# An attention and feed-forward kernel whose instruction order is planned: three edits to the attention units, one to a buffer, and a table of offsets to the planner's ranks

## The chip, the cores and the metric

The kernel runs on one core of one Trainium2 chip, in one launch. The metric is the device time of that launch in microseconds (us), timed in three runs. TensorE is called PE here, VectorE DVE, ScalarE ACT, GpSimd POOL, and SyncE, which issues most DMAs, SP.

## The reference

Attention over 4 batches of 8 heads, 768 positions of width 64. A query sees the 8 first keys ("global") and the last 96 keys up to itself ("local"), with a bias that falls with distance. The heads are laid side by side to 3072 tokens of 512 values, and a feed-forward follows.

```python
scores = scale * np.matmul(q, k.transpose(0, 1, 3, 2))
scores = np.where(keep, scores + bias, -1000000000.0)
a = np.exp(scores - np.max(scores, axis=-1, keepdims=True))
a = a / (np.sum(a, axis=-1, keepdims=True) + 1e-09)
x = np.matmul(a, v)            # heads side by side: (3072, 512)
h = x @ w_in                   # (512, 2048), doubles
g = h * np.cos(h)
out = g @ w_out                # (2048, 512), doubles
```

The two weight matrices come as 64-bit floats.

## The kernel before, in words

**Tiling.** The tokens are cut into chunks: two of 384 tokens for the first batch (chunks 0 and 1, four blocks of 96 each), then for each further batch two of three blocks and one of two (chunks 2 to 10; 4, 7 and 10 have two blocks). Every chunk has four attention units, one for each pair of heads. After attention, each chunk goes through the feed-forward in steps over the 2048 hidden columns: chunks 0 and 1 in 16 steps of 128 columns each (chunk 0 does four, chunk 1 all sixteen, chunk 0 the rest), the others in eight steps of 256. The first product of a step is "M1" (line 973); it lands in one of two PSUM banks (`ph`), and ACT, DVE, ACT, DVE make h*cos(h) of it (turn 991, angle 994, cosine 997, product 1030 or 1096), then a rounded part and a rest. The second product is line 986 for chunks 0 to 2, and from chunk 3 on a form with seven block products instead of eight (line 1191), which reads sums of the output weights that are kept in DRAM and streamed back. Each matmul of a product is done as three of rounded parts and rests.

**An attention unit.** PE makes the scores (663 or 667), DVE copies the causal half over (685) and takes bias and minimum (694), ACT takes the exponential with its sum (719), DVE adds 1e-9 and takes the reciprocal (727, 730), POOL divides (743, 748), PE transposes (847, two blocks at a time), and the transposed weights go from PSUM to SBUF as two tiles: one for the product with the preceding block's keys and the global ones, one for the own block's. Then PE multiplies by the values (890): the "burst", whose matmuls use 64 of the array's columns, two side by side. ACT or DVE copies the result to `xmem` (297, 299), DVE the rest (938). In chunks named in `DIFFER` (4 to 10) the first tile is a plain copy by ACT or DVE (`every`), and the burst takes differences of neighbouring value blocks (`vd`, line 821) with the second tile; in the others DVE masks the first tile (`others`, line 858) and no differences are made. Two-block chunks put two head pairs into one burst; `MERGE` names further chunks that do so, and is empty.

**The order.** Nothing runs in source order. Every operation is put on a list with its possible engines, its estimated cost, what it waits for, which buffers it uses and, for some, a time by which it is due. The planner gives every operation a rank (`o.key`, its latest start; line 158) and then walks through time: a free engine takes the ready operation of lowest rank whose buffers are free, a choice among engines going by waiting time and cost. The program holds each engine's instructions in that order, so each engine's queue is fixed. The planner's cost of one M1 part is 348 ns, a burst's 160 ns for each pair of matmuls; a change of array form costs 170 ns. In the first 45 us of planned time PE's gaps are filled with matmuls on zeros ("idle<-zeros", line 1518), 250 ns each.

**Buffers that matter here.** From chunk 4 on, attention has two of the eight PSUM banks for scores, transposes and burst results (`att`); chunks 2 and 3 have three. A chunk's finished rows wait in an SBUF tile `oo` for the DMA to the output; before chunk 3 that tile is taken from the class `wu` (two places, shared with weight conversion and the sums), afterwards from `oo` (two places).

Of the kernel before, what the change touches and what calls it, by code (L numbers as in the profile page):

```python
# [26 lines left out]
R = 96  # L27
# [39 lines left out]
MERGE = tuple(range(11, 11))  # L67
DIFFER = tuple(range(4, 11))
# [3 lines left out]
TAIL = 0.8  # L72

# [32 lines left out]
class Plan:  # L106
# [12 lines left out]
    def __init__(self, places, free):  # L119
        self.ops = []  # L120
        self.places = {c: list(v) for c, v in places.items()}
        self.busy = {}
        self.free = dict(free)
        self.port = 0
        self.mode = None
        self.last = {}

# [5 lines left out]
    def op(self, engines, emit, after=(), uses=(), due=None, table=None, extra=0, port=False, mode=None):  # L133
        o = Op(engines, emit, after, list(uses), due, table, extra, port, mode)
        for a in o.after:
# [137 lines left out]
class Net:  # L273
# [143 lines left out]
    def plan_weight(self, src, out, at, place, n, due):  # L417

        nc, p = self.nc, self.plan
        raw = Slot(f"w {place}", lambda i: self.const.tile([P, n, 2], U32, name="raw", tag=i))  # L420
# [53 lines left out]
        o = p.op({DVE: part(600)}, wjoin, [o], [raw, wu], port=True)  # L474
        o = p.op({ACT: part(525), DVE: part(335), POOL: part(595)}, whigh, [o], [raw, wu], port=True)
        return p.op({DVE: part(600), POOL: part(1260)}, wrest, [o], [raw, wu], due=due, port=True)

    def plan_combined(self, q):
# [11 lines left out]
        done = [[x] + self.prev.get("sums", []) for x in done]  # L490
# [99 lines left out]
    def plan_unit(self, L, pr):  # L590
# [134 lines left out]
        def add(e):  # L725
            x = st.tile[:, n2 : 2 * n2]
            nc.vector.tensor_scalar(x, x, 1e-9, None, op0=ALU.add)

        def rec(e):
            nc.vector.reciprocal(st.tile[:, 2 * n2 : 3 * n2], st.tile[:, n2 : 2 * n2])  # L730
# [69 lines left out]
    def plan_values(self, u):  # L800
# [18 lines left out]
        def step(e):  # L819
            x = vs.tile[:R, :, hs]  # L820
            self.eng(e).tensor_tensor(
                vd.tile[:, pos + lead0 : pos + nb], x[:, lead0 + 1 : nb + 1], x[:, lead0:nb], op=ALU.subtract)
# [6 lines left out]
        for ts in u["groups"]:  # L829
# [37 lines left out]

            def whole(e, pt=pt, pv=pv):
# [8 lines left out]
            ready.append(p.op({DVE: 70 + w * 104 // 100}, own, [o], [pt, pv]))  # L877
# [28 lines left out]
        def burst(e):  # L906
# [4 lines left out]
            {PE: 160 * (2 * nb - u["first"]) * len(units)}, burst, [o for x in units for o in x[3]],  # L911
# [87 lines left out]
    def plan_step(self, s, m, q, a, b):  # L999
# [10 lines left out]
        for i in range(2):  # L1010
            f = 2 * q + i
            for kk in range(self.NK):

                def m1(e, kk=kk, f=f, i=i):
# [3 lines left out]
                    {PE: 348}, m1, self.xdone[m, kk] + [self.wdone[f][0]], [ph, *xs, self.weight["wi", f]],  # L1018
# [100 lines left out]
    def plan_fast(self, s, m, q, rr, gg, product, g, due):  # L1119
# [54 lines left out]
        for i, (bank, half, left, right, k) in enumerate(jobs):  # L1174
# [12 lines left out]
            def times(e, b=b, half=half, left=left, right=right, ends=half == 1 or bank == "D"):  # L1187
# [7 lines left out]
                {PE: 348}, times, after, uses + side, due=due + (i + 1) * 348,  # L1195
# [65 lines left out]
    def plan_store(self, m, t, po, o, keep, due):  # L1261
# [5 lines left out]
        else:  # L1267
            cls = "part" if keep else "wu" if m < FAST else "oo"
# [176 lines left out]
    def windows(self):  # L1445
# [17 lines left out]
        self.weight, self.saved, self.stored = {}, {}, {}  # L1463
        p = self.plan
# [13 lines left out]
        for n in self.order:  # L1478
            for b2 in range(self.NP // UB):
                L = self.plan_loads(n, b2)  # L1480
                for i in range(UB):
                    self.plan_values(self.plan_unit(L, b2 * UB + i))
        for f in range(self.NF):
            self.wdone[f] = self.plan_weights(f)
        for q in range(NQ):
            self.plan_combined(q)
        for s, (n, i, a, b) in enumerate(self.seq):
            (self.plan_opening if n < len(OPEN) else self.plan_step)(s, n, i, a, b)
        flag = self.plan_flag()
# [105 lines left out]
```

## Time and profile before

| | |
|---|---|
| timed runs | 678.24 us median of 3 (677.9 to 679.14) |
| span of the profiled execution | 676.7 us, first to last instruction |
| what lies around the span, by the median | 1.6 us |
| busy | PE 663.8, PE weight loads 626.7, DVE 554.6, ACT 508.7, POOL 391.0 us |
| granted TensorE clock | 0.998 of full speed over the span |

Busy time of an engine is what its records cover. Matmuls overlap: a matmul of 256 columns has a record of about 280 ns, but the next one starts some 117 ns after it. So PE's busy share says that something was in the array, not that matmuls started as fast as they could; for that one reads the starts in the timeline. The profile's own span and the timed median differ by 1.6 us of launch and end.

### The profile page before, as it was taken

The numbers are of one execution on the slowest core, as the hardware profiler recorded it, in microseconds if no ns is written. First come the engines' busy times: TensorE is split into PE (matmuls) and PEld (weight loads), VectorE is DVE, ScalarE is ACT, GpSimd is POOL, SyncE is SP. The second block draws the span as 40 slices with busy tenths as digits, with TensorE's granted clock in tenths as the row PEclk, the third lists the DMA queues.
The fourth block names the chain that finished last, engine by engine and source line by source line (L and its number), as shares of the span: only waits on it lengthen the run. The fifth ranks groups of instructions, "written<-read, shape, count | busy, mean of one in ns | idle before, by whom it ended". The sixth has DMA issues, their size and how long they took to land. (4 is left out here: it accounts for less than half of the span.)

```text
span 676.7 us, 17496 instructions
## 1 busy us (share of the span) xinstructions
PE 663.8 (98%) x5810; PEld 626.7 (93%) x5810; DVE 554.6 (82%) x1726; ACT 508.7 (75%) x1253; POOL 391.0 (58%) x576
## 2 busy tenths in 40 slices
PE   8999999999999999999999999999999999999995
PEld 4769999999999998999999999999999999999995
DVE  7999898978898897777778888797878898887664
ACT  7999997579776785866778878676787788684432
POOL 5896544437457553467866776736876768532201
PEclk9999999999999999999999999999999999999999
DMA  8999200044546665877887867787687777665664
GB/s 279 336 321 380 80 1 1 22 159 121 163 139 194 221 183 174 239 220 203 244 240 207 249 213 231 245 239 232 210 240 219 235 228 235 199 224 187 191 226 150
DMA packets 86291, 136.69 MB, mean 202 GB/s; under 512 B 9904, under 2 KB 33968, under 8 KB 86192
## 3 DMA queue, kind: packets, MB, share of 16 engines
q1 hardware_dynamic: 86048, 135.23, 64.7%
q8 instruction: 48, 0.79, 0.5%
q14 instruction: 51, 0.42, 0.2%
q10 hardware_dynamic: 144, 0.26, 0.1%
HBM read 118.67 MB, written 16.78 MB: 200 GB/s over the span
## 5 line engine op out<-in xcount | busy, mean ns | idle before, releaser
L973 PE MATMUL bank<-xmem,w 128*128 128x256 f32 (+1 forms) x2112 | 344.4, 295 | 0.1
L973 PEld LDWEIGHTS bank<-xmem,w 128*128 128x128 f32 x2112 | 294.1, 189 | 7.7 <-issue 0.9
L719 ACT ACTIVATE tt<-tt,st 96x104 f32<-96x104 f32 (+1 forms) x256 | 94.6, 371 | 7.2 <-DVE st L694 6.5
L997 ACT ACTIVATE rr<-rr,half_pi 128x512 f32<-128x512 f32 (+1 forms) x104 | 71.6, 691 | 23.3 <-DVE rr L994 22.1
L986 PE MATMUL bank<-w,gh 128*128 128x256 f32 (+1 forms) x384 | 88.3, 320 | 0.0
L991 ACT ACTIVATE rr<-bank 128x512 int32<-128x512 f32 (+1 forms) x104 | 57.9, 558 | 30.9 <-PE bank L973 29.1
L1191 PE MATMUL bank<-ws,sh 128*128 128x256 f32 x384 | 75.8, 284 | 1.3 <-DVE oo L299 1.3
L994 DVE SCALAR_TENSOR_TENSOR rr<-rr,bank 128x512 f32<-128x512 int32 (+1 forms) x104 | 66.5, 639 | 8.2 <-ACT rr L991 7.6
L784 POOL TENSOR_TENSOR qk<-raw,qk 64x304 fp32r<-64x304 f32 (+1 forms) x57 | 50.0, 880 | 28.4 <-ACT qk L297 6.9
L748 POOL TENSOR_TENSOR tt<-tt,st 96x416 f32<-96x416 f32 (+1 forms) x60 | 45.4, 764 | 35.3 <-DVE sf L1137 9.1
L986 PEld LDWEIGHTS bank<-w,gh 128*128 128x128 f32 x384 | 62.7, 188 | 1.1
L1030 DVE TENSOR_TENSOR rr<-bank,rr 128x512 f32<-128x512 f32 x72 | 49.3, 684 | 16.6 <-ACT rr L997 16.4
L986 PE MATMUL bank<-w,gl 128*128 128x256 f32 (+1 forms) x192 | 61.1, 318 | 0.0
L1191 PEld LDWEIGHTS bank<-ws,sh 128*128 128x128 f32 x384 | 58.6, 188 | 2.0 <-issue 1.4
L297 ACT CAST gh<-rr 128x384 fp32r<-128x384 f32 (+1 forms) x76 | 39.5, 520 | 25.8 <-DVE rr L1030 10.8
L694 DVE CUSTOM_DVE_ANT_0 tt<-bank,dd 96x104 f32<-96x104 f32 (+1 forms) x256 | 55.0, 256 | 2.2
L1191 PE MATMUL bank<-ws,sl 128*128 128x256 f32 x192 | 54.1, 282 | 0.1
L997 ACT ACT_TABLE_LOAD x40 | 51.3, 1283 | 0.7
L719 ACT ACT_TABLE_LOAD x39 | 50.0, 1283 | 0.7
L445 POOL TENSOR_SCALAR raw<-raw 128x512 bf16<-128x512 bf16 (+1 forms) x32 | 36.6, 1167 | 23.6 <-DVE w L466 13.2
L667 PE MATMUL bank<-qk 128*96 128x200 f32 (+1 forms) x384 | 49.1, 257 | 0.0
L1191 PE MATMUL bank<-w,gh 128*128 128x256 f32 x256 | 48.7, 282 | 0.0
(137 smaller groups left out, 1532.4 us busy)
## 6 DMA issues: line engine op xcount, KB each, us to landing
ws<-sum SPq DMA_DIRECT2D x256, 256.0 KB
raw<-in_qk_dram SPq DMA_DIRECT2D x48, 174.0 KB
raw<-in_w_in_dram SPq DMA_DIRECT2D x16, 512.0 KB
sum<-sw SPq DMA_DIRECT2D x64, 128.0 KB
raw<-in_qk_dram SPq DMA_DIRECT2D x48, 150.0 KB
raw<-in_qk_dram SPq DMA_DIRECT2D x48, 148.0 KB
out_dram<-oo SPq DMA_DIRECT2D x23, 256.0 KB
raw<-in_w_out_dram SPq DMA_DIRECT2D x16, 256.0 KB
```

Of the source, the lines that this page charges most:

```text
L667: nc.tensor.matmul(out, qs[:, m, q0], ks[:, k : k + w], start=m == 0, stop=m == 1)
L694: nc.vector.tensor_tensor_reduce(tt[t // 2].tile[:, t % 2, j, :w], ps.tile[:R, i * WIN : i * WIN + w], self.dd[:, v, :w], op0=ALU.add, op1 ...
L719: nc.scalar.activation(x, x, AF.Exp, bias=st.tile[:, c : c + 1], scale=-1.0, accum_out=st.tile[:, n2 + c : n2 + c + 1])
L748: self.eng(e).tensor_tensor(x, x, r.broadcast_to([R, na, SLOT]), op=ALU.mult)
L784: self.eng(e).tensor_tensor(ks[D:, k0:k1], raw.tile[D:, k0:k1], ks.bitcast(F32)[D:, k0:k1], op=ALU.subtract)
L973: self.nc.tensor.matmul(ph, self.wi[f][:, w, kk * P : (kk + 1) * P], xx[:, kk, :], start=kk == 0 and m == 0, stop=kk == self.NK - 1 and m ...
L986: self.nc.tensor.matmul(out, gg, w[:, i, :], start=start and m == 0 and h == 0, stop=stop and m == 2)
L991: self.nc.scalar.activation(r.bitcast(I32), ph, AF.Copy, scale=1.0 / TWO_PI, bias=0.25)
L994: self.nc.vector.scalar_tensor_tensor(r, r.bitcast(I32), -TWO_PI, ph, op0=ALU.mult, op1=ALU.add)
L997: self.nc.scalar.activation(r, r, AF.Sin, bias=self.half_pi)
L1030: {DVE: dve(512)}, lambda e: nc.vector.tensor_tensor(r(), h(), r(), op=ALU.mult), [o], [ph, rr],
L1191: nc.tensor.matmul(out, x, y, start=q == 0 and j == 0 and half == 0, stop=q == self.NF // 2 - 1 and j == 2 and ends)
```

## The change

It does six things. (1) `MERGE` names chunks 2 to 10, so their three-block units also go two head pairs to a burst. (2) `DIFFER` takes in chunks 0 and 1: they make value differences and copy the first tile plainly. (3) In chunks 0 and 1 (`APART`) the add and the reciprocal are done for each pair of blocks, not once a unit. (4) Chunk 2's output tile comes from `oo`, not `wu`. (5) The planner's costs: 354 for an M1 or second-product part, 168 for a pair of burst matmuls; the first weight sums wait for the 24th-last weight that was joined. (6) Each operation has a name, and a table of 615 offsets (in ns) is added to the ranks. `COPIED` is empty, so its code does nothing.

```diff
-MERGE = tuple(range(11, 11))
-DIFFER = tuple(range(4, 11))
+BEHIND = -24
+MERGE = tuple(range(2, 11))
+DIFFER = (0, 1) + tuple(range(4, 11))
+COPIED = ()
+APART = (0, 1)
+ORDER = {
+    "u0.0 high": -45860, "v0.1 glob": -1510, "u0.1 fold": -540, "u0.1 exp": -28590, "u0.1 op2": 810,
...
+}
-            o.key = (o.due - min(o.engines.values()), i)
+            o.key = (o.due - min(o.engines.values()) + ORDER.get(o.name, 0), i)
-        done = [[x] + self.prev.get("sums", []) for x in done]
+        done = [[x] + self.prev.get("sums", self.joined[BEHIND:]) for x in done]
-        o = p.op({DVE: 85}, add, exps, [st], port=True)
-        o = p.op({DVE: 120}, rec, [o], [st], port=True)
+        ends = None
         u["norm"] = []
         for ts in groups:
             h, na = ts[0], 2 * len(ts)
+            if n in APART or ends is None:
+                cs = (2 * h, 2 * h + na) if n in APART else (0, n2)
+                ends = [x for ((t, _), _), x in zip(ttr, exps) if t in ts or n not in APART]
+                o = p.op({DVE: 85}, lambda e, cs=cs: add(e, *cs), ends, [st], port=True)
+                o = p.op({DVE: 120}, lambda e, cs=cs: rec(e, *cs), [o], [st], port=True)
-            {PE: 160 * (2 * nb - u["first"]) * len(units)}, burst, [o for x in units for o in x[3]],
+            {PE: 168 * (2 * nb - u["first"]) * len(units)}, burst, [o for x in units for o in x[3]],
-            cls = "part" if keep else "wu" if m < FAST else "oo"
+            cls = "part" if keep else "wu" if m < FAST - 1 else "oo"
```

**PE, two neighbouring units of chunk 5.** Before, each head pair has its own burst (890; `vd` are the value differences), with first products (973) and second products (1191) between:

```order
L973 MATMUL bank<-xmem,w 128x256 x6
L890 MATMUL bank<-pv,v 64x96 x4
L890 MATMUL bank<-pv,vd 64x96 x2
L890 MATMUL bank<-pv,v 64x96 x2
L890 MATMUL bank<-pv,vd 64x96 x2
L973 MATMUL bank<-xmem,w 128x256 x6
L1191 MATMUL bank<-ws,gh 128x256 x2
L1191 MATMUL bank<-ws,gl 128x256
L973 MATMUL bank<-xmem,w 128x256 x12
L667 MATMUL bank<-qk 96x96 x2
```

After, the same chunk (1031 is the burst, 1332 the second product):

```order
L1332 MATMUL bank<-w,gl 128x256
L1031 MATMUL bank<-pv,v 64x96 x4
L1031 MATMUL bank<-pv,vd 64x96 x2
L1031 MATMUL bank<-pv,v 64x96 x2
L1031 MATMUL bank<-pv,vd 64x96 x2
L1031 MATMUL bank<-pv,v 64x96 x4
L1031 MATMUL bank<-pv,vd 64x96 x2
L1031 MATMUL bank<-pv,v 64x96 x2
L1031 MATMUL bank<-pv,vd 64x96 x2
L1332 MATMUL bank<-w,gh 128x256 x2
L1332 MATMUL bank<-w,gl 128x256
```

Two units' ten matmuls each stand in one run of twenty (the trace has two records for each of them). Over the whole program the runs of burst matmuls go from 38 to 26. Eighteen second-product matmuls follow this one before the next scores. Of the matmuls on zeros 48 become 34; all other counts on PE stay.

**ACT, the middle of the opening.** Before (435 is a weight conversion, 991 and 997 turn and cosine, 719 the exponentials, 297 copies: `gh` the rounded part of h*cos(h), `xmem` attention's result):

```order
L991 ACTIVATE rr<-bank 128x384 x2
L435 ACTIVATE raw<-raw 128x512
L997 ACT_TABLE_LOAD
L997 ACTIVATE rr<-rr,half_pi 128x384
L297 CAST xmem<-bank 128x384
L719 ACT_TABLE_LOAD
L719 ACTIVATE tt,st<-tt,st 96x104 x8
L297 CAST gh<-rr 128x384
L997 ACT_TABLE_LOAD
L997 ACTIVATE rr<-rr,half_pi 128x384
L719 ACT_TABLE_LOAD
L719 ACTIVATE tt,st<-tt,st 96x104 x8
```

After (1138 cosine, 848 exponentials, 424 copies, 563 a weight conversion; `pv` are the transposed weights):

```order
L848 ACTIVATE tt,st<-tt,st 96x104 x3
L1138 ACT_TABLE_LOAD
L1138 ACTIVATE rr<-rr,half_pi 128x384
L424 CAST w<-wu 128x512
L848 ACT_TABLE_LOAD
L848 ACTIVATE tt,st<-tt,st 96x104
L424 COPY pv<-bank 104x384
L848 ACTIVATE tt,st<-tt,st 96x104 x6
L424 COPY pv<-bank 104x384
L848 ACTIVATE tt,st<-tt,st 96x104
L563 ACTIVATE raw<-raw 128x512
L848 ACTIVATE tt,st<-tt,st 96x104 x3
```

One excursion to the cosine is gone and copies of `pv` stand between the exponentials. Counted up to the 64th exponential, the last of chunks 0 and 1, ACT has 14 copies of `pv` more (ten of 104x384, four of 104x192) and one of `xmem` more; it has two table loads, two scalings of the queries, one turn, one cosine and three conversions of line 435 (one of 512, two of 256 columns) fewer. Up to the same chunks' last `xmem` rest, DVE loses all 16 masked copies of line 858 (twelve 104x384, four 104x192) and gains five `vd` and eight more pairs of add and reciprocal; POOL gains three `vd`.

## Rows read from the trace of the kernel before

**Rows 1.** First part of the page: busy us (share of the span) xinstructions

```profile
PE 663.8 (98%) x5810; PEld 626.7 (93%) x5810; DVE 554.6 (82%) x1726; ACT 508.7 (75%) x1253; POOL 391.0 (58%) x576
```

**Rows 2.** Windows: stretch, its us, then each engine's busy time, clock, DMA

```profile
12.00:62.00 50.00, 48.28 (x499) 36.47 (x500) 46.48 (x205) 49.71 (x163) 41.53 (x49) 1.00 0.99 345
62.00:100.00 38.00, 38.00 (x227) 35.98 (x227) 33.74 (x59) 38.00 (x87) 19.29 (x19) 1.00 0.28 93
100.00:200.00 100.00, 99.99 (x716) 93.84 (x715) 86.36 (x247) 77.71 (x182) 49.26 (x69) 1.00 0.31 96
```

**Rows 3.** Waits of PE after 60 us: total us, times, longest

```profile
PE bank L1191 <- DVE oo L299: 1.3, 1, 1.3
PE bank L847 <- DVE pv L299: 0.7, 1, 0.7
```

**Rows 4.** Timeline of PE around one three-block burst: start, us, what

```profile
364.18 0.40 PE L1191 MATMUL bank<-ws,gh 128*128 128x256 f32 x2
364.42 0.28 PE L1191 MATMUL bank<-ws,gl 128*128 128x256 f32 x1
364.62 0.39 PE L890 MATMUL bank<-pv,v 104*64 104x96 f32 x4
364.84 0.34 PE L890 MATMUL bank<-pv,vd 96*64 96x96 f32 x4
...
365.77 0.99 PE L973 MATMUL bank<-xmem,w 128*128 128x256 f32 x6
366.60 0.54 PE L667 MATMUL bank<-qk 128*96 128x200 f32 x4
```

**Rows 5.** Timeline of PE around a burst that holds two head pairs

```profile
423.14 0.39 PE L890 MATMUL bank<-pv,v 104*64 104x96 f32 x4
...
424.62 0.63 PE L973 MATMUL bank<-xmem,w 128*128 128x256 f32 x3
```

**Rows 6.** Timeline of DVE and of SP's queue before 270 us

```profile
269.27 0.69 DVE L299 COPY oo<-bank 128x512 f32<-128x512 f32 x1 [1.92 <-DMA out_dram<-oo]
...
264.66 5.69 SPq L1283 DMA_DIRECT2D out_dram<-oo  x2
```

**Rows 7.** Timeline of PE: fillers in the opening, and what follows

```profile
8.49 3.41 PE L1518 MATMUL idle<-zeros 128*128 128x512 bf16 x15
12.05 0.51 PE L847 MATMUL bank<-ident,tt 96*96 96x96 f32 x4
```

**Rows 8.** Groups by form, first 80 us: busy us, mean ns

```profile
L858 DVE SCALAR_TENSOR_TENSOR pv<-own,bank 104x384 f32<-104x384 f32 x12 | 6.5, 545 | 0.4 <-PE bank L847 0.3
L618 ACT ACTIVATE raw<-raw,steep 128x384 f32<-128x384 f32 x7 | 4.3, 615 | 3.7 <-POOL small L357 2.8 <-DMA raw<-in_qo_dram 0.8
L435 ACT ACTIVATE raw<-raw 128x512 int32<-128x512 uint32 x18 | 11.6, 680 | 0.0
L435 ACT ACTIVATE raw<-raw 128x256 int32<-128x256 uint32 x8 | 3.3, 432 | 0.0
L997 ACT ACTIVATE rr<-rr,half_pi 128x384 f32<-128x384 f32 x8 | 4.9, 616 | 0.0
L991 ACT ACTIVATE rr<-bank 128x384 int32<-128x384 f32 x9 | 4.3, 487 | 0.0
L297 ACT CAST xmem<-bank 128x384 fp32r<-128x384 f32 x6 | 2.8, 464 | 0.0
L997 ACT ACT_TABLE_LOAD x3 | 3.8, 1283 | 0.1
```

**Rows 9.** Groups by form, whole span: ACT's copies of the transposed weights

```profile
L297 ACT COPY pv<-bank 104x384 f32<-104x384 f32 x15 | 7.1, 476 | 3.7 <-DVE pv L864 3.6
L297 ACT COPY pv<-bank 104x192 f32<-104x192 f32 x18 | 5.4, 318 | 4.7 <-PE bank L847 2.5 <-DVE pv L864 2.0
```

**Rows 10.** Instructions of the value differences on DVE

```profile
L821 DVE TENSOR_TENSOR vd<-v x1: 543/543/543, 538.8 to 538.8; 96x384 f32<-96x384 f32 x1
```

**Rows 11.** Timeline of DVE after the burst of Rows 4

```profile
366.97 0.52 DVE L938 TENSOR_TENSOR xmem<-bank,xmem 128x224 fp32r<-128x224 f32 x2
```

More of the change, by code (lines that the diff above doesn't have):

```diff
@@ L126, in __init__ @@
         self.last = {}
+        self.part, self.count = "", {}
     def drained(self, o, e):
@@ L134, in op @@
         o = Op(engines, emit, after, list(uses), due, table, extra, port, mode)
+        name = emit.__name__
+        if name == "<lambda>":
+            self.count[self.part] = self.count.get(self.part, 0) + 1
+            name = f"op{self.count[self.part]}"
+        o.name = f"{self.part} {name}"
         for a in o.after:
@@ L419, in plan_weight @@
         nc, p = self.nc, self.plan
+        p.part = place
         raw = Slot(f"w {place}", lambda i: self.const.tile([P, n, 2], U32, name="raw", tag=i))
@@ L723, in plan_unit, with add, rec @@
             exps.append(p.op({ACT: 365}, exp, [o], [tt[t // 2], st], table="exp"))
-        def add(e):
-            x = st.tile[:, n2 : 2 * n2]
+        def add(e, a, b):
+            x = st.tile[:, n2 + a : n2 + b]
             nc.vector.tensor_scalar(x, x, 1e-9, None, op0=ALU.add)
-        def rec(e):
-            nc.vector.reciprocal(st.tile[:, 2 * n2 : 3 * n2], st.tile[:, n2 : 2 * n2])
-        o = p.op({DVE: 85}, add, exps, [st], port=True)
-        o = p.op({DVE: 120}, rec, [o], [st], port=True)
+        def rec(e, a, b):
+            nc.vector.reciprocal(st.tile[:, 2 * n2 + a : 2 * n2 + b], st.tile[:, n2 + a : n2 + b])
+        ends = None
         u["norm"] = []
@@ L821, in step @@
             self.eng(e).tensor_tensor(
-                vd.tile[:, pos + lead0 : pos + nb], x[:, lead0 + 1 : nb + 1], x[:, lead0:nb], op=ALU.subtract)
+                vd.tile[:, pos + lead0 : pos + nb], x[:, lead0 + 1 - low : nb + 1 - low], x[:, lead0 - low : nb - low], op=ALU.subtract)
         w = (nb - lead0) * P
@@ L866, in own, with mine @@
                 )
+            def mine(e, pv=pv, a=a, na=na, z0=z0):
+                self.eng(e).tensor_tensor(
+                    wide(pv.tile[:R, 1, z0:], a, na), wide(pv.tile[:R, 0, z0:], a, na), mask(self.own[:R], a, na), op=ALU.mult
+                )
             def whole(e, pt=pt, pv=pv):
@@ L876, in plan_values @@
                 ready.append(p.op({DVE: 70 + w * 104 // 100}, others, [o], [pt, pv]))
-            ready.append(p.op({DVE: 70 + w * 104 // 100}, own, [o], [pt, pv]))
+            if n in COPIED:
+                ready.append(p.op({DVE: 70 + w * 104 // 100, POOL: 100 + w * 1125 // 512}, mine, ready[-1:], [pv], port=True))
+            else:
+                ready.append(p.op({DVE: 70 + w * 104 // 100}, own, [o], [pt, pv]))
             if lead:
@@ L1017, in plan_step @@
                 done = self.chain(f"m1 {s}", p.op(
-                    {PE: 348}, m1, self.xdone[m, kk] + [self.wdone[f][0]], [ph, *xs, self.weight["wi", f]],
+                    {PE: 354}, m1, self.xdone[m, kk] + [self.wdone[f][0]], [ph, *xs, self.weight["wi", f]],
                     due=due + (4 * i + kk + 1) * 348,
@@ L1194, in plan_fast @@
             last[bank, half] = self.chain("m2", p.op(
-                {PE: 348}, times, after, uses + side, due=due + (i + 1) * 348,
+                {PE: 354}, times, after, uses + side, due=due + (i + 1) * 348,
             ))
```

8 lines of the change are left out of this document (added), and 114 rows, old and new, of the table ORDER.

## The prediction

> **What bounds the kernel now.** I read the first part of the page first: PE is busy for 663.8 of 676.7 us [rows 1], so only what PE itself does, or the few microseconds in which it does nothing useful, can move the time. The windows then say where the others matter [rows 2]. From 12 to 62 us ACT is busy for 49.71 of 50 us and DVE for 46.48, while PE has time for fillers: this is the opening, in which attention for the first batch and the conversion of the weights both press on ACT. From 62 to 100 us PE and ACT are both full; from 100 us PE alone (99.99 of 100, ACT 77.71). The table of waits, restricted to the time after 60 us, has little: one wait of 1.3 us and one of 0.7 us that count [rows 3]. A busy PE can still be slow, so I read starts in its timeline last, around a change of array form: that is where a cost hides inside "busy" [rows 4, 5].
>
> **Bursts (a gain of 4.2 us).** Take the burst of one head pair in a three-block chunk [rows 4]. From its first start at 364.62 to the next full-width matmul at 365.77 are 1.15 us for 24 records. A burst of two head pairs with two blocks each has 32 records and takes 424.62 - 423.14 = 1.48 us [rows 5]. The eight records between them cost 0.33 us, 0.041 each, so 24 of them are 0.99 us and 0.16 us is a fixed part; the longer burst has the same (1.48 - 32 x 0.041 = 0.16): a second pair in the burst pays nothing. Around it, two plain matmuls take 364.42 - 364.18 = 0.24, 0.12 each, but the last before the burst takes 0.20, which is 0.08 too much, and the six after it take 366.60 - 365.77 = 0.83 instead of 0.72, 0.11 too much. One run of burst matmuls thus costs 0.16 + 0.08 + 0.11 = 0.35 us beyond its matmuls. Runs go from 38 to 26. Twelve times 0.35 is 4.2 us, all of it on PE after 100 us, where PE is full, so nothing hides it. Bounds: if only the fixed part inside goes, 12 x 0.16 = 1.9; at most 4.2 plus what the runs' neighbours cost, which I leave at 4.6.
>
> **Chunk 2's output tile (1.3 us).** The longest wait of PE after 60 us is that on the copy `oo` by DVE [rows 3]. DVE's own timeline shows why it is late: the copy at 269.27 waited 1.92 us for a DMA from `oo` to the output, one of the pair that SP's queue starts at 264.66 [rows 6]. Its place was still being sent. With `oo` this chunk has two places of its own class that no sum or weight uses, so the second copy needs not wait for the first one's DMA. I take all 1.3 us; the lower bound is 0, if another operation of `oo` comes as late.
>
> **The opening (0.5 us).** Here the edits add and remove much, so I count each queue up to the last opening exponential or rest, from the counts in the order. ACT gains ten `pv` copies of 384 columns at 0.476 and four of 192 at 0.318 [rows 9], 6.0 us, and one `xmem` copy, 0.46. It loses two table loads, 2 x 1.283 = 2.57, two query scalings, 1.23, a turn and a cosine, 0.49 + 0.62, and three conversions, 0.68 + 2 x 0.43 = 1.54 [rows 8]; together 6.45. The queue that is never idle is as long as before, so the last opening exponential comes when it came, and what follows on ACT with it. DVE loses 12 x 0.545 = 6.5 us of masked copies alone [rows 8] and gains five `vd`, one at 0.543 [rows 10] and four that are a third wider, about 0.7 each by estimate from it, 3.3 in all; eight more pairs of tiny add and reciprocal take most of the rest. The transposes need each half's reciprocal only, so the first half of a unit reaches PE earlier, and fewer gaps open: the planner puts 14 fewer fillers. In the trace 15 fillers and the way to the next transpose take 12.05 - 8.49 = 3.56 us, 0.237 each [rows 7], so 14 are 3.3 us. That is the upper bound of the gain. It can't all stay, because PE's first products hand over to ACT through two banks, and ACT's queue has not become shorter: what PE gains at 50 us it waits for ACT by 75 us. The other bound is a loss: a `pv` copy on ACT can stand at the head of the queue and wait. Over the span 33 such copies of these two shapes sat idle for 3.7 + 4.7 us [rows 9], 0.25 each; fourteen of them would cost 3.6 us. Between a gain of 3.3 and a loss of 3.6 I take a gain of 0.5, since DVE's shorter queue brings the copies' partners earlier.
>
> One rule speaks against moving `vd` to DVE. The Trainium skill, page "SBUF — State Buffer", section "SBUF: two separate sides", says that VectorE and GpSimd share one port pair as an exclusive lock, taken for a whole instruction by a VectorE operation with two inputs in SBUF, and `vd` is one. By it five `vd` would hold POOL for about 3.3 us while POOL divides. The rows show POOL with 8.5 us of 50 idle there [rows 2], and no `vd` on DVE in the opening; no run here shows the lock by itself. By the rule the opening's gain would be gone, and the sum 0.5 smaller.
>
> **Ranks (0.5 us).** The offsets reorder PE after 100 us: first products run further ahead of their second products, so angle, cosine and sums have more time. What is left there to gain by the waits is 0.7 us [rows 3], plus small ones that no row of that view holds. I take 0.5; bounds are a gain of 2.5 us and a loss of 2.5, since a new order can put an operation before its input. The costs 354 and 168 only shape the plan. The copies of `xmem` that a merged burst brings all come at once, on ACT and DVE that have 22 and 14 us of 100 idle [rows 2].
>
> **The sum.** 4.2 + 1.3 + 0.5 + 0.5 = 6.5 us off a span of 676.7 is 670.2. The median of the timed runs is 1.6 us above the span, 678.24. With the same 1.6 us, the prediction is 671.7.
>
> **Rivals.** *The opening's gain stays.* If ACT's copies find their transposes ready and PE keeps its 3.3 us, and the 0.7 us of [rows 3] goes too, the time is 678.24 - 4.2 - 1.3 - 3.3 - 0.9 = 668.5. For it: 14 fillers fewer; against it: ACT's 49.71 of 50 [rows 2]. Chance 0.18.
>
> *The merged bursts give it back.* From chunk 4 on a merged burst takes both attention banks, and no scores or transposes can start until the copies are out. In the trace a bank is free at 366.97 + 0.52 = 367.49, 1.7 us after PE went on at 365.77 [rows 4, 11]; two pairs need two more copies, another 0.5 us. In the order 18 second-product matmuls at 0.12 stand behind the burst shown, 2.1 us, and at some bursts fewer. If PE waited 0.5 us after each of 12, 6.0 us would come back and with the rest of the sum unchanged it would be 677.7: no change. Against it: PE has enough other work in between at most places. Chance 0.09.
>
> *Slower: ACT's copies block the opening.* A `pv` copy and DVE's masked copy read the same bank, and the copy waits for the other: 3.6 us before the 15 wide ones [rows 9]. If each of the 14 new ones waits for a transpose and for DVE, with its own length, 0.476 + 0.25 = 0.73 us, and the two table loads and the rest that pay for them in my count were waited for anyway, ACT is 14 x 0.73 = 10.2 us late at 62 us, and PE, fed by ACT's turns through two banks, is too. 678.24 - 4.2 - 1.3 + 10.2 = 682.9. It decides the sign from a net delay of about 7 us on. For it: ACT is full to 100 us. Against: the same copies as a mask stood on DVE, itself nearly full, and the table loads do go. Chance 0.07.
>
> *The lock* of the paragraph above, as a mechanism: POOL's divisions wait for DVE's `vd`, five times about 0.66 us, and the gain of the opening turns into a loss of 0.5: 672.7. Chance 0.06.
>
> **How the numbers follow.** The forecast has 0.60, with its own range 668.9 to 674.5. A change of 0.2%, 1.36 us, is about what can be told from none. Faster than 676.9: the forecast, the first rival and the lock, 0.84, and a part of the second, 0.02, so 0.86. Within 0.2%: the rest of the second rival, 0.07. Slower: 0.07. The range for 8 in 10 goes from 667.0, a bit below the first rival by the upper bounds of ranks and bursts, to 676.8, where the bounds of opening and ranks, 3.6 and 2.5 lost, would leave 678.24 - 4.2 - 1.3 + 3.6 = 676.3 with ranks at 0.
>
> **What would show it.** Bursts: 26 runs of burst matmuls, a run of 40 records taking about 40 x 0.041 + 0.16 = 1.8 us, and the matmul after it starting as before. Output tile: no wait of PE on `oo` near 270 us, and no wait of DVE on a DMA there. Opening: the 64th exponential within 1.5 us of where it was, 34 fillers, ACT still full from 12 to 62 us, and PE's saturation not earlier by more than 2 us. Ranks: waits of PE after 60 us below 1.5 us in all. I am wrong if scores or transposes wait for a bank after merged bursts, if ACT has idle time before `pv` in the opening, or if PE is seen waiting between 62 and 100 us for ACT.

## The result and the profile after

The changed kernel takes 686.19 us (median; 685.21 to 686.93) against 678.31 us of the kernel before in the same session: a ratio of 1.0113, 95% interval 1.0098 to 1.0127. It is slower by 7.9 us where 6.5 us less were forecast. The profiled execution has a span of 684.6 us against 676.7.

The first part of the page of the changed kernel answers [rows 1]:

```profile
PE 664.1 (97%) x5796; PEld 629.8 (92%) x5796; DVE 554.4 (81%) x1737; ACT 505.8 (74%) x1263; POOL 396.1 (58%) x579
```

Every engine's work is what it was, within some 5 us (PE 663.8 to 664.1, ACT 508.7 to 505.8, POOL 391.0 to 396.1). What grew is PE's idle time, span less busy: from 12.9 to 20.5 us, nearly all of the loss. That PE's busy time did not fall, with 14 fillers fewer and twelve bursts joined, is in part the halved clock described below, under which its matmuls take longer. The windows say where. They answer [rows 2]; the columns are the stretch and its us, busy us of PE, PEld, DVE, ACT and POOL with instructions, PE's granted clock, the DMA share, GB/s.

```profile
12.00:62.00 50.00, 45.91 (x467) 35.41 (x464) 42.84 (x202) 47.31 (x165) 33.20 (x42) 0.93 0.97 319
62.00:100.00 38.00, 37.50 (x222) 35.01 (x222) 34.79 (x63) 37.66 (x84) 15.38 (x16) 1.00 0.38 127
100.00:200.00 100.00, 99.48 (x697) 93.29 (x697) 87.28 (x239) 77.74 (x197) 60.95 (x77) 1.00 0.31 96
...
300.00:400.00 100.00, 97.42 (x914) 95.55 (x913) 83.23 (x274) 77.91 (x197) 63.52 (x96) 1.00 0.78 226
...
500.00:600.00 100.00, 97.43 (x930) 94.99 (x929) 83.07 (x257) 74.93 (x173) 58.49 (x83) 1.00 0.77 223
```

The two last stretches in the kernel before, same columns:

```profile
300.00:400.00 100.00, 99.10 (x935) 96.41 (x935) 78.55 (x263) 77.16 (x201) 72.11 (x117) 1.00 0.75 222
...
500.00:600.00 100.00, 100.00 (x950) 98.22 (x949) 84.97 (x267) 78.52 (x196) 69.88 (x104) 1.00 0.78 232
```

Two losses are to be seen. In the opening ACT, which had 0.3 us of 50 idle, has 2.7, and PE's clock is 0.93 instead of 1.00. And late in the program, in the two stretches shown, PE stands idle 2.6 us of 100, where it had been idle for 0.9 and not at all. From 200 to 300 us it is the other way round (1.5 us idle before, none now); over 100 to 600 us PE's idle time goes from 2.4 to 6.4 us.

**How much of it is the opening.** A count of what PE has done by 100 us tells: the windows from 0 to 100 us for one line alone (columns: busy PE, busy PEld, clock, DMA share, GB/s; the weight loads lose no record, so I count these). First products in the kernel before and in the changed one:

```profile
0.00:100.00 100.00, 35.10 (x167) 28.96 (x168) 1.00 0.70 236
```

```profile
0.00:100.00 100.00, 29.28 (x147) 25.14 (x147) 0.97 0.73 237
```

Second products stand at 135 in both. So 21 first products are missing at 100 us. One starts 0.177 us after another: in the timeline of PE before, six take 83.39 - 82.33 = 1.06 us.

```profile
82.33 1.22 PE L973 MATMUL bank<-xmem,w 128*128 128x384 f32 x6
83.39 0.40 PE L986 MATMUL bank<-w,gh 128*128 128x256 f32 x2
```

That is 21 x 0.177 = 3.7 us lost by 100 us. The other 7.9 - 3.7 = 4.2 us are lost later, in the part where bursts and the output tile should have given 4.2 + 1.3 = 5.5 us back. If they did, about 9.7 us of new waiting stands against them. The table of waits that follows holds 5.9 of these (6.8 us after 100 us, less the 0.9 that stood beside the `oo` wait before), so this sum does not show that the whole 5.5 us came.

**Which waits.** PE's waits after 60 us in the changed kernel, answering [rows 3] (total us, times, longest):

```profile
PE bank L1114 <- DVE rr L1171: 1.5, 3, 0.7
PE bank L1031 <- ACT pv L424: 1.2, 2, 0.8
PE bank L796 <- ACT pv L424: 1.2, 1, 1.2
PE bank L796 <- DVE pv L426: 0.7, 1, 0.7
PE bank L980 <- POOL tt L881: 0.6, 1, 0.6
PE bank L1127 <- ACT oo L424: 0.5, 1, 0.5
PE bank L796 <- POOL qk L917: 0.5, 2, 0.3
```

Before there were two waits that counted, 2.0 us together; the seven rows here sum to 6.2 us, all rows of that view to 7.3, and name scores (L796), bursts (L1031), transposes (L980) and first products (L1114), behind ACT, DVE and POOL. There is no single culprit. The wait on `oo` in chunk 2 is gone, as forecast.

One of these waits, followed back, shows how the new order makes them. PE, ACT and SP's queue before 398 us in the changed kernel:

```profile
393.21 0.49 PE L980 MATMUL bank<-ident,tt 96*104 96x96 f32 x4
...
397.59 0.58 PE L796 MATMUL bank<-qk 128*96 128x200 f32 x4 [1.16 <-ACT pv L424]
```

```profile
395.30 0.45 ACT L424 CAST qk<-raw 128x304 fp32r<-128x304 f32 x1 [2.86 <-DMA raw<-in_qk_dram]
...
396.97 0.47 ACT L424 COPY pv<-bank 104x384 f32<-104x384 f32 x1
```

```profile
384.45 2.81 SPq L1298 DMA_DIRECT2D ws<-sum  x5
387.48 2.39 SPq L900 DMA_DIRECT2D raw<-in_qk_dram  x4
```

Scores need a bank that holds transposed weights until ACT has copied them. The transposes ran at 393.21, but the copy only at 396.97: it stood in ACT's queue behind a conversion of `qk`, which waited 2.86 us for its load; and that load was issued behind transfers of `ws` (five in the window shown). PE waits for ACT, ACT for a DMA that has nothing to do with the copy. By the Trainium skill, page "TensorE: Matmul & The Clock Gate", section "Architectural detail: the array is 16× 32×32, not 1× 128×128", the queues of ACT and DVE are strictly first in, first out; the copy that could run and did not agrees.

**The clock.** PE's timeline at 51 us shows the burst of 32 records that should take 1.48 us:

```profile
50.55 0.51 PE L980 MATMUL bank<-ident,tt 96*104 96x96 f32 x4 [0.38 <-DVE st L823]
51.44 0.39 PE L1031 MATMUL bank<-pv,v 104*64 104x96 f32 x4 [0.38 <-ACT pv L424]
...
53.46 0.54 PE L1031 MATMUL bank<-pv,vd 96*64 96x96 f32 x4
54.16 1.04 PE L1127 MATMUL bank<-w,gh 128*128 128x256 f32 x2 [0.16 <-ACT w L424]
```

Here it takes 54.16 - 0.16 - 51.44 = 2.56 us up to the end of its last record (1.56 by that count at 423 us in the kernel before). The granted clock of 52 to 58 us is 0.50, the lower of the two levels (1.2 GHz). Ahead of it PE had stood before bank after bank from 46 us on, and of the fillers 34 are left of 48, the last at 41.9 us instead of 44.3.

**The bursts themselves** did what was forecast. A joined one of 48 records in the changed kernel, answering [rows 4, 5]:

```profile
374.13 0.39 PE L1031 MATMUL bank<-pv,v 104*64 104x96 f32 x4
374.34 0.34 PE L1031 MATMUL bank<-pv,vd 96*64 96x96 f32 x4
...
376.28 1.56 PE L1114 MATMUL bank<-xmem,w 128*128 128x256 f32 x11
```

It takes 376.28 - 374.13 = 2.15 us; 48 x 0.041 + 0.16 is 2.13. The fixed part is paid once for two pairs. Its neighbours cost what they did: in the four bursts of 48 records that have full-width matmuls on both sides and no wait, the matmul ahead takes 0.21 us and the six behind 0.81, by their starts. The timeline has 26 runs of burst matmuls.

### The profile page after: what moved, and what is told of

It is laid out like the page before. It is cut to its first block, busy times and chain, and to the rows that moved or that the text cites. A ratio compares the mean times of both kernels' runs of the same rounds, so it can differ in the third digit from the quotient of the medians.

```text
span 684.6 us, 17411 instructions
## 1 busy us (share of the span) xinstructions
PE 664.1 (97%) x5796; PEld 629.8 (92%) x5796; DVE 554.4 (81%) x1737; ACT 505.8 (74%) x1263; POOL 396.1 (58%) x579
## 4 chain that ended last, share of the span: by engine, by line
PE 72%; DVE 8%; ACT 8%; DMA 6%; POOL 3%; issue 2%; SPq 0%; POOLq 0%; ACTq 0%; DVEq 0%
PE bank L1114 32%; PE bank L1332 17%; PE bank L1127 13%; DMA raw<-in_qk_dram 4%; PE bank L796 4%; PE bank L1031 3%; ACT tt L848 2%; PE bank L980 2%; DMA v<-in_v_dram 1%; ACT pv L424 1%; DVE tt L823 1%; DVE bank L814 1%; DVE qk L907 1%; POOL qk L917 1%; DVE pv L997 1%
## 5 line engine op out<-in xcount | busy, mean ns | idle before, releaser
L1114 PE MATMUL bank<-xmem,w 128*128 128x256 f32 (+1 forms) x2112 | 309.0, 295 | 1.5 <-DVE rr L1171 1.5
L1114 PEld LDWEIGHTS bank<-xmem,w 128*128 128x128 f32 x2112 | 281.7, 189 | 5.7 <-PE bank L796 0.8
L1332 PE MATMUL bank<-ws,sh 128*128 128x256 f32 x384 | 73.7, 284 | 0.0
L917 POOL TENSOR_TENSOR qk<-raw,qk 64x304 fp32r<-64x304 f32 (+1 forms) x60 | 54.1, 907 | 28.5 <-DVE qk L907 3.4
L1127 PEld LDWEIGHTS bank<-w,gh 128*128 128x128 f32 x384 | 64.4, 192 | 5.6 <-ACT oo L424 0.9
L1171 DVE TENSOR_TENSOR rr<-bank,rr 128x512 f32<-128x512 f32 x72 | 49.0, 684 | 14.2 <-ACT rr L1138 13.8
L428 POOL TENSOR_SCALAR sh<-sf 128x512 fp32r<-128x512 f32 x43 | 27.4, 637 | 47.3 <-PE bank L1332 19.6
L814 DVE COPY_PREDICATED bank<-mine,bank 96x192 f32<-96x192 uint32 (+1 forms) x128 | 40.2, 327 | 15.0 <-PE bank L796 14.2
L796 PE MATMUL bank<-qk 128*96 128x200 f32 (+1 forms) x384 | 47.7, 257 | 3.2 <-ACT pv L424 1.2
```

Source lines behind the costliest of these rows:

```text
L796: nc.tensor.matmul(out, qs[:, m, q0], ks[:, k : k + w], start=m == 0, stop=m == 1)
L814: nc.vector.copy_predicated(w[:, :, :R], self.mine.bitcast(U32).broadcast_to([R, ni - i0, R]), w[:, :, SLOT:])
L917: self.eng(e).tensor_tensor(ks[D:, k0:k1], raw.tile[D:, k0:k1], ks.bitcast(F32)[D:, k0:k1], op=ALU.subtract)
L1114: self.nc.tensor.matmul(ph, self.wi[f][:, w, kk * P : (kk + 1) * P], xx[:, kk, :], start=kk == 0 and m == 0, stop=kk == self.NK - 1 and m ...
L1127: self.nc.tensor.matmul(out, gg, w[:, i, :], start=start and m == 0 and h == 0, stop=stop and m == 2)
L1171: {DVE: dve(512)}, lambda e: nc.vector.tensor_tensor(r(), h(), r(), op=ALU.mult), [o], [ph, rr],
```

## The experiments

The theories: **A**, the table of offsets puts operations ahead of their inputs. **B**, the joined bursts cost by what they hold (two banks, copies of two pairs at once). **C**, the opening's edits cost. **D** came after the first four runs: the plan of before is a rarely good one, and any new order, with or without a reason, opens waits that the old one had not. All times are medians of device us; ratios are to the kernel before, run beside it, with 95% intervals.

### Parts of the change alone

`no_table`: the changed kernel with an empty table.

```
-    "u0.0 high": -45860, "v0.1 glob": -1510, "u0.1 fold": -540, "u0.1 exp": -28590, "u0.1 op2": 810,
...
+ORDER = {}
```

> The changed kernel with an empty table of offsets; every other edit is in it. Theory A (the offsets cost the time: they put scores, first products and bursts ahead of their inputs, so that PE waits): the bursts' 4.2 us and the output tile's 1.3 us show, and the time is 671 to 674 us. Theory B (the merged bursts cost it, because scores and transposes wait for the banks that two head pairs hold): 682 to 686, as in the changed kernel. Theory C (the opening costs it, by value differences and sums per half unit): 681 to 685, with the granted clock of 12 to 62 us again below 1.00.

684.01 us, ratio 1.0078 (1.0064 to 1.0092). Most of the loss is there without the table. A is refuted as the main cause; the offsets account for some 2 us. The time fits both B and C, but C's clock does not: it is 1.00 from 12 to 62 us.

`merge_oo`: the kernel before with two lines of the diff.

```
-MERGE = tuple(range(11, 11))
+MERGE = tuple(range(2, 11))
-            cls = "part" if keep else "wu" if m < FAST else "oo"
+            cls = "part" if keep else "wu" if m < FAST - 1 else "oo"
```

> The kernel before with two of the edits alone: two head pairs share a burst from batch two, and chunk 2's output tile has a place of its class. No table, no new costs, the opening as before. Theory A and theory C: 12 x 0.35 + 1.3 = 5.5 us less than before, 672.8, and no wait of PE on an output copy near 270 us. Theory B: no gain, 677 to 682, with PE's scores and transposes waiting for a bank after bursts of 40 or 48 records.

682.74 us, 1.0066 (1.0052 to 1.008): 3.8 us slower, where the parts promise 5.5 less, and just above B's range. The opening is as before (168 first products by 100 us), so what is lost, 9.3 us if both terms came in full, is lost later, by joining and planning anew. PE's waits after 60 us sum to 6.6 us, against 2.2 before; they name POOL's `tt`, DVE's `rr` and `qk`, again many small ones.

`open_only`: the opening's edits alone.

```
-DIFFER = tuple(range(4, 11))
+DIFFER = (0, 1) + tuple(range(4, 11))
+APART = (0, 1)
```

> The kernel before with the opening's edits alone: value differences for the first two blocks, and sums per half unit there. Theory C: 680 to 684, with fewer fillers, PE idle from 45 to 60 us and a granted clock under 1.00 there. Theories A and B: 677 to 679, the clock 1.00 from 12 to 62 us; by the prediction's term 677.7.

682.52 us, 1.0056 (1.004 to 1.0071). The time is C's, the clock (1.00) is not: PE is idle more, without a fall. By 100 us PE had done 159 first products instead of 168, and 130 second ones instead of 135.

`table_late`: the changed kernel, the offsets of the opening left out: the names that begin with `u0`, `u1`, `v0`, `v1`, `w`, `c0` and `s0` to `s19`.

```
-    "u0.0 high": -45860, "v0.1 glob": -1510, "u0.1 fold": -540, "u0.1 exp": -28590, "u0.1 op2": 810,
...
     "v2.0 glob": -12810, "u2.0 op1": -76810, "u2.0 op2": -70080, "u2.0 khigh": -18650, "u2.0 op3": -31250,
```

> The changed kernel with the offsets of the opening left out (units and values of the first two blocks, weights, the first sum, steps 0 to 19); all later ones stay. Theory A, if the loss comes from the later offsets: 681 to 686, with PE's waits after 130 us as in the changed kernel (scores and bursts behind ACT's and DVE's copies). If it comes from the opening's offsets: 673 to 677. Theory B gives 682 to 686 in either case, theory C 681 to 685 with the clock below 1.00 in the opening.

693.95 us, 1.0219 (1.0204 to 1.0233), outside every range. Part of the table is worse than none and worse than all of it, which suggests that the offsets fit each other and the order that they make together. This, and that both parts alone (`merge_oo`, `open_only`) lose some 3.7 us, pointed to D. The delay of the first weight sums (edit 5; the code makes them wait for all of the last 24 joined weights, not for the 24th-last) was not run alone.

### The order held

To part an edit from the plan that comes with it, I wrote the plan of the kernel before down (each operation's engine and rank) and let the kernel follow that list instead of the planner. An operation whose shared bank or buffer is still taken goes next after that is free. That the order is held can be read from `held_oo` below: in its trace PE, DVE, ACT and POOL run every instruction in the order of the kernel before.

```
-        self.emit(p.run(), banks)
+        self.emit(p.replay(), banks)
```

`held_merge` has the held order and `MERGE` of the change.

> The kernel before with its whole order held by a written list (each operation with the engine and the rank that it has in the kernel before) and one edit: two head pairs share a burst from batch two, the first pair's burst records moved down to the second pair's. Nothing else moves but what the joined burst pushes back. Theory D (the edits do what they say; it is the new plan, in any version, that opens waits which the old one had not): 12 x 0.35 = 4.2 us less than before, 673 to 676. Theory B (the merged burst itself costs, by banks and copies that it holds): 677 to 682, with waits of transposes or scores right behind bursts of 40 and 48 records.

692.98 us, 1.0205 (1.0191 to 1.0218): 14.2 us slower. Both ranges are missed by far. Joining moves the first pair's copies down by the distance of two bursts, on top of the second pair's, and nothing else makes room. The opening is as before (168 first products by 100 us). DVE's waits between 130 and 670 us, in the kernel before and in this one:

```profile
DVE xmem L938 <- ACT xmem L297: 3.5, 7, 0.9
```

```profile
DVE xmem L2214 <- ACT xmem L1558: 13.7, 17, 1.6
```

`held_merge_oo` adds the output tile.

> The same held order with the joined bursts and chunk 2's output tile in its own class. Theory D: the two terms add, 5.5 us less than before, 672 to 674.5, faster than both kernels. Theory B: 676 to 681.

690.65 us, 1.0167 (1.0153 to 1.0181). The tile gives 2.3 us here too; the joined bursts cost the rest.

`held_oo`: the held order, the output tile alone.

> The held order of the kernel before, and the output tile's class alone. Under every theory the wait on the output copy near 270 us goes and nothing else changes: 1.3 us less than before. If the next operation of that tile is as late: no difference.

676.98 us, 0.9976 (0.9966 to 0.9987), the only version faster than before, and so faster than both kernels. PE's waits after 60 us have only one row left:

```profile
PE bank L2114 <- DVE pv L1560: 0.7, 1, 0.7
```

`cost_only`: no edit, the planner's two costs alone.

```
-                    {PE: 348}, m1, self.xdone[m, kk] + [self.wdone[f][0]], [ph, *xs, self.weight["wi", f]],
+                    {PE: 354}, m1, self.xdone[m, kk] + [self.wdone[f][0]], [ph, *xs, self.weight["wi", f]],
```

(the same for second products, and 168 for 160 at the burst)

> A control without any of the edits: the kernel before with the planner's costs for a group of full-width matmuls and for a burst at the new values alone. The same operations in another order. Theory D: 680 to 684, as the other new plans. Theories A, B and C name no reason for a change: 677.5 to 680.

688.58 us, 1.0137 (1.012 to 1.0155), above D's range too. The same operations in another order are 9.8 us slower, more than the whole change. By 100 us it had 139 first products and 108 second ones, against 168 and 135. The first products alone make 29 x 0.177 = 5.1 us, all lost in the opening, and the second ones come on top. The clock of 12 to 62 us was 0.93 in the profiled execution. Two of the four executions have a clock of 0.999 over their span and take 687.5 and 687.7 us, so 8.9 us of the loss are there at that clock.

### A neutral order, and the order of the change

`jitter`: no edit, a random offset on each rank.

```
-            o.key = (o.due - min(o.engines.values()), i)
+            o.key = (o.due - min(o.engines.values()) + some.randint(-500, 500), i)
```

> A control without any of the edits: the kernel before, where each operation's rank gets a random offset of at most 0.5 us either way, one fixed draw. Theory D (the plan of before is one of the best among plans that look alike to the planner; a neutral new one loses some microseconds, by the waits that it happens to open): 680 to 688. Theory B (the joined bursts make the loss, the plan as such little): 677.5 to 680. The control with the two new costs gave 688.6, most of it in the opening; if the present one gives 678 to 680, those costs and not the new order were the reason there.

686.41 us, 1.0104 (1.0085 to 1.0122). D's range holds it, B's does not. Its opening is intact (167 first products); it loses after 100 us. Two of its six executions have a clock of 0.998 and more, against 0.995 or 0.996 in the others, and take 683.9 and 684.7 us: some 5 us of the loss are there at the full clock. The window from 100 to 400 us in the kernel before and here:

```profile
100.00:400.00 300.00, 297.58 (x2530) 283.69 (x2529) 248.95 (x763) 227.72 (x551) 175.30 (x257) 1.00 0.58 175
```

```profile
100.00:400.00 300.00, 294.43 (x2485) 280.13 (x2483) 241.17 (x732) 223.90 (x539) 187.94 (x262) 0.99 0.57 172
```

Its largest waits of PE stand behind POOL's `qk`, although POOL is idle for over a third of that stretch:

```profile
PE bank L683 <- POOL qk L804: 3.2, 3, 1.5
```

`held_swap`: as `held_merge`, with another order of the copies after a joined burst; chunk 8 (pair and copy):

```
-0 high1, 0 high2, 0 rest1, 0 rest2, 1 high1, 1 high2, 1 rest1, 1 rest2
+0 high1, 0 high2, 1 high1, 1 high2, 1 rest1, 0 rest1, 1 rest2, 0 rest2
```

In its trace eight of the twelve joined bursts have all high parts ahead of the first rest; at the other four a first rest stays ahead.

> The held order of before with joined bursts, as in the first such run (693.0), but the copies behind a joined burst in another order: the high parts of both pairs first, then the rests of both. In the first run DVE stood 13.7 us, 17 times, before a rest for ACT's high part, against 3.5 us, 7 times, in the kernel before. If that queueing of copies behind a joined burst is the reason: these waits fall below 7 us and the time to 684 to 688. If it is the two banks that the burst holds, or the late loads of the values, it stays at 691 to 694.

689.04 us, 1.015 (1.0137 to 1.0163): 3.9 us better, between the two answers. DVE's waits before rests halve, to the 7 us that the expectation had as its bound:

```profile
DVE xmem L2216 <- ACT xmem L1560: 7.0, 13, 1.5
```

So queueing of copies is a part, some 4 of 14 us. Other waits came instead: DVE's for PE's scores go from 7.6 to 13.4 us, and PE now waits for the rests, which hold its banks longer:

```profile
PE bank L1932 <- DVE xmem L2216: 2.1, 4, 0.6
```

More buffers for `v`, `vd` or `pv` were not tried.

`after_split`: the changed kernel with its own order held and the twelve bursts split again.

```
-MERGE = tuple(range(2, 11))
+MERGE = tuple(range(11, 11))
-        self.emit(p.run(), banks)
+        self.emit(p.replay(), banks)
```

> The reverse: the changed kernel with its own order held, and its joined bursts split again; the first pair's burst goes six ranks behind its last input, its copies behind it, all else stays. If joining costs more by waits than it saves by array forms (theory B): 680 to 685, below the changed kernel. If the joined bursts keep their 4.2 us and the rest of the new plan loses (theories A and D): 688 to 692.

700.26 us, 1.0341 (1.0305 to 1.0378): 14 us slower than the changed kernel, far outside both ranges. Joining cost 14 us in the order made for single bursts, splitting cost 14 us in the order made for joined ones. That tells more of orders than of bursts.

`after_fill`: the changed kernel, fillers allowed until 60 us.

```
-FILL_TO, FILL_REST, FILL_EACH, FILL_FIRST, FILL_COLD = 45000, 150, 250, 10, 7000
+FILL_TO, FILL_REST, FILL_EACH, FILL_FIRST, FILL_COLD = 60000, 150, 250, 10, 7000
```

> The changed kernel in its own order, with ten more fillers for PE, all between 45 and 60 us, where its granted clock fell to half. If the fallen clock cost what the trace shows (a burst of 58 records took 2.7 instead of 1.5 us, and what followed it): the granted clock of 12 to 62 us is 0.98 or more and the time 684 to 685.5. If the waits behind the copies set the end of the opening and the clock only filled them: the clock is 1.00 and the time as in the changed kernel, 685.5 to 687.

685.25 us, 1.0096 (1.0082 to 1.0111). The clock of 12 to 62 us is back at 1.00, also around the burst:

```profile
12.00:62.00 50.00, 46.46 (x483) 34.25 (x480) 43.88 (x203) 48.29 (x168) 34.53 (x43) 1.00 0.99 322
50.00:54.00 4.00, 3.69 (x45) 2.20 (x42) 3.06 (x16) 3.51 (x14) 2.21 (x4) 1.00 1.08 271
```

(The expectation's 58 records are a miscount; that burst has 32.) By 100 us 154 first products are done instead of 147, 7 x 0.177 = 1.2 us. The medians differ by 0.9 us, with intervals of the ratios that overlap. The changed kernel's own four executions agree: one had a clock of 0.999 over its span and took 685.21 us, the three with 0.992 took 686.02 to 686.93. So the clock is about 1 us of the opening's 3.7. It is not the cause of the rest: with the clock restored, PE still starts no first product from 46 to 58 us, as in the changed kernel.

### What joined bursts are worth among new orders

Pairs with the same random draw of ranks by operation name, once with single and once with joined bursts, all with the new output tile.

```
+            some = random.Random(f"1 {o.name}").randint(-500, 500)
```

> The kernel before with chunk 2's output tile in its own class and a random offset of at most 0.5 us on each rank, drawn by the operation's name, draw 1; bursts single as before. By the control without that tile (686.4), 680 to 688.

> The same draw 1 with joined bursts. Theory D (joined bursts keep their gain where the plan is new anyway): 2 to 4.2 us below the partner with single bursts. Theory B (by waits they cost what they save, or more): equal or above it.

> Draw 2 of the random offsets, bursts single: 679 to 688 us, by the control with another draw (686.4) less what the output tile gives.

> Draw 2, bursts joined. Theory D: 2 to 4.2 us below its partner with single bursts; theory B: equal or above it.

> Draw 3 of the random offsets, bursts single, chunk 2's output tile in its own class: 680 to 690 us, as the two draws before it (689.8 and 689.2).

> Draw 3, bursts joined. Theory D: 2 to 4.2 us below its partner with single bursts, as draws 1 and 2 (1.7 and 3.7 below); theory B: equal or above it.

| draw | single: us, ratio | joined: us, ratio |
| --- | --- | --- |
| 1 | 689.83, 1.0148 (1.0119 to 1.0178) | 688.15, 1.0156 (1.0118 to 1.0194) |
| 2 | 689.23, 1.0166 (1.0136 to 1.0196) | 685.54, 1.0096 (1.0078 to 1.0115) |
| 3 | 689.31, 1.0155 (1.0137 to 1.0173) | 694.88, 1.0239 (1.0195 to 1.0283) |

By the ratios the joined bursts make no difference that can be told, gain 0.7% (4.7 us) and lose 0.8% (5.7 us); by the medians they are 1.7 and 3.7 us below and 5.6 above. (The ratios go by means and without the profiled execution, hence the difference.) Neither D's "2 to 4.2 us below" nor B's "equal or above" holds in all three, and draws 1 and 2 with single bursts lie above their ranges. The joins save PE's changes of form; what they are worth net is open: it drowns in the luck of the order. All five orders without the change's edits to attention (`jitter`, `cost_only` and the three singles, which have the output tile) are 7 to 11 us slower than the kernel before.

## Why the prediction was wrong

**Ranks: the step that failed.** It took 0.5 us gain, with bounds of 2.5 us either way, because the rows of the old trace had only 0.7 us left to win. But a wait that is not in the trace of before has no row there, and a new order can open any number of them. How wide the bound had to be is what a neutral order shows: 7.3 us lost for at most half a microsecond of noise on the ranks, 9.8 us for two costs that the prediction dismissed as "only shape the plan" (5 and 8.9 us in their executions with the higher clock). The sign that it had named, waits of PE after 60 us below 1.5 us in all, came out at 7.3. The table itself cost some 2 us. The same holds for the other edits, since each of them plans the whole kernel anew: their terms were summed as if the rest stayed where it was. How the change's 7.9 us divide among its edits is not shown, since each edit came with an order of its own. With DVE busy for 82% of the span and PE for 98%, the old order was fitted to within 2.0 us of such waits of PE [rows 3]. The forecast took that fit as given for every new order too.

**Bursts: mechanism right, net value lost.** Runs, length, fixed part and the cost of the neighbours came as worked out. The 4.2 us are not to be seen in the total of any of these kernels: `merge_oo` is 3.8 us slower. The rival "the merged bursts give it back" named waits behind the copies and got the kind right where the order was held (DVE's 13.7 us before ACT's copies in `held_merge`, PE's 2.1 us on `xmem` in `held_swap`), with 677.7 too little. Its price was 0.5 us after each burst; the waits stood elsewhere too, at first products and transposes behind DVE's `rr` and POOL's `tt`.

**Output tile: right.** 1.3 us were forecast, 1.8 measured in the held order (0.9 to 2.3 by the interval), and the wait is gone.

**Opening: the sign was wrong, the size just outside the bound.** A loss of 3.7 us by 100 us against a gain of 0.5, with a bound of 3.6 lost. My count of ACT's queue up to the 64th exponential came out even, and so far it was right: that exponential ends at 53.1 us instead of 52.9. The step that failed is "and what follows on ACT with it". The two table loads, the turn and the cosine that I took off the queue were not saved but moved behind that exponential; over the whole program both kernels have 40 table loads for cosines and 39 for exponentials. ACT's second cosine ran at 47.99 us, amid the exponentials; in the changed kernel it runs at 57.09:

```profile
47.99 0.62 ACT L997 ACTIVATE rr<-rr,half_pi 128x384 f32<-128x384 f32 x1
```

```profile
57.09 0.62 ACT L1138 ACTIVATE rr<-rr,half_pi 128x384 f32<-128x384 f32 x1
```

First products hand over to ACT and DVE through two banks. DVE reads such a bank for its product after that cosine, at 58.49 us, and PE starts its next first product at 59.19. First products counted as above, before (first row) and in the changed kernel (the other two):

```profile
0.00:58.00 58.00, 10.23 (x48) 8.09 (x48) 1.00 0.95 318
```

```profile
0.00:46.00 46.00, 8.04 (x36) 6.01 (x36) 1.00 0.92 298
0.00:58.00 58.00, 8.10 (x36) 6.01 (x36) 0.95 0.95 302
```

The changed kernel stands at 36 first products from 46 to 58 us, while the kernel before went from 24 to 48: 12 of the 21 that are missing at 100 us. That the late cosine is what holds them is read from the order of the two queues; no run moved it alone. Of the signs I had named, "ACT has idle time before `pv`" came true: of its 2.7 us (47.31 of 50 busy instead of 49.71) 2.0 stand before copies of `pv`, most of that behind DVE's copy of the own block:

```profile
ACT pv L424 <- DVE pv L997: 1.6, 3, 0.9
```

PE was also seen waiting for ACT between 62 and 100 us, though only once and for 0.5 us. Fewer fillers, which I read as gaps closed, also left PE without cover, and the clock fell: about 1 us. The slower rival (ACT's `pv` copies late by 10 us) had the sign right, and its wait is there, but not its size: ACT was not late at the 64th exponential and not full, and the waits of PE's bursts on `pv` up to 60 us are four, of at most 0.5 us, 1.7 us in all. The lock of the port pair was not tested by itself. But `open_only` too is a new plan; whether its 3.6 us belong to the value differences or to the order can't be told apart by these runs.

Two figures of the forecast do not follow from their own text: the first rival takes off 0.9 us where it names 0.7, and the range's upper end, 676.8, leaves out the 2.5 us of the ranks' bound, with which its sum would be 678.8.

What a table of offsets could bring was shown from the other side: with all offsets 686.2, with none 684.0, with the late ones alone 694.0.

## What to carry to other kernels

When an edit goes through a planner, price the new order first: run the old kernel with a neutral change of order, and if that costs more than the edit promises, as here (7 to 10 us against 6.5), the sum of terms says nothing about the total. Hold the order and change one thing; an edit that needs no room (the output tile) keeps its gain, 1.8 us, and one that moves a pair's copies on top of another's loses 14. The absence of waits in a tuned trace is no slack: in the changed kernel one late load was passed on, at 397 us, through ACT's queue to a copy that had nothing to do with it. And an operation that a count finds gone from one stretch must be looked for in the next: the cosine that left the opening's exponentials came 9 us later, and PE's first products with it.

## What the runs showed of the hardware

The fall of PE's clock is not decided by the order alone. Executions of one and the same kernel differ: the changed kernel had a clock of 0.999 over its span once and 0.992 three times, and the one took 685.2 us where the three took 686.4 in the mean. In `cost_only` two executions had 0.999 (687.6 us in the mean) and two 0.994 (690.0); in `jitter` two had 0.998 and 0.999 (684.3) and four 0.995 or 0.996 (687.0). So the executions with the lower clock took 1.2 to 2.7 us longer.

Draw 1 shows the same in the traces: both of its kernels run the same instructions in the same order up to 147 us. In the kernel with single bursts the clock halves after 54 us, in the one with joined bursts, with less PE work just before, it stays (single first, then joined):

```profile
50.00:54.00 4.00, 2.32 (x27) 1.50 (x22) 3.69 (x19) 3.96 (x11) 3.51 (x5) 1.00 0.93 302
54.00:58.00 4.00, 3.69 (x35) 3.46 (x36) 3.58 (x11) 4.00 (x16) 1.95 (x5) 0.51 0.91 318
```

```profile
50.00:54.00 4.00, 2.01 (x20) 1.27 (x16) 3.68 (x18) 3.96 (x13) 3.52 (x5) 1.00 0.89 293
54.00:58.00 4.00, 3.93 (x44) 3.45 (x44) 3.58 (x10) 4.00 (x16) 1.94 (x5) 1.00 0.99 334
```

A fall can so cost a microsecond or two in one execution and be absent from the next, and a profile shows only one of them.
